# Turning attention weights two slots back instead of one in the opening of a top-k attention and MLP kernel

## The chip, the cores and the metric

The kernel runs on one core of a Trainium2 chip. The metric is the time of the device in microseconds, from the first instruction to the last, of one launch. Before the change it is 1626.51 us, the median of three runs (1626.12 to 1628.27). The profile is of another execution of the same kernel, whose span is 1627.3 us.

The core has five engines with a queue of instructions each: TensorE (PE in the profile; its weight loads are shown apart, as PEld), VectorE (DVE), ScalarE (ACT), GpSimd (POOL) and SyncE (SP, which here only starts transfers). [...]

## The reference

Two blocks, one after the other. First, attention that keeps the 32 largest scores of each row:

```python
B, H, S, D = 8, 8, 576, 64
scores = 1/sqrt(D) * q @ k.transpose(0, 1, 3, 2)
kth    = 32nd largest of each row
scores = where(scores >= kth, scores, -1e9) - max
attn   = exp(scores) / (sum(exp(scores)) + 1e-9)
x      = (attn @ v) as (4608 tokens, 512)
```

Then a two-layer MLP over the 4608 tokens, with w_in (512 x 2048) and w_out (2048 x 512):

```python
h   = x @ w_in
g   = h * sigmoid(1.702 * h)
out = g @ w_out
```

All of it is in 32-bit floats.

## The kernel before, in words

**Tiling.** A batch has 8 heads, taken as 4 pairs, and 576 rows, taken as four blocks of 128 and one of 64. A unit of attention work is 128 rows of two heads (the 64-row ends of two pairs share one unit). There are 18 units in a batch, so N = 144 in all; unit and slot have the same number n. The 128 lanes hold rows in the search, and the score row of a head has 576 columns.

**The stages of a unit**, by name and line:

- prepare (L199 to L208): TensorE transposes q and k, ScalarE copies the result out of PSUM.
- scores (L231): eight passes on TensorE into two PSUM tiles; copy_scores (L242): ScalarE copies them to SBUF, tile by tile.
- topk (L251, L254): VectorE finds the 32 largest of each row in four rounds of MAX8, with MATCH_REPLACE8 between them: 14 operations of two heads.
- bounds (L270, L271): GpSimd works out two small values from the largest and the 32nd largest.
- exponentials (L279, L281): ScalarE, two passes for each head; the second also sums the row.
- divide (L290, L292, L296): VectorE takes the reciprocal of the sum after the sixth operation of the next unit's search. For units below 11, GpSimd makes from it two diagonal matrices (the tile "by"), and turning then divides as it transposes.
- turn_main and turn_ends (L312, L315; L310 from unit 11 on): TensorE transposes the exponentials, in two main parts of 512 columns and one of 128; ScalarE copies each part to SBUF (L320).
- values (L342): TensorE multiplies by v; ScalarE copies the result (L354) into the token block xT. Four units complete a token block, which then is "ready".
- hidden (L385): a quarter of the first MLP layer of a ready block; tanh (L402) on ScalarE; gate (L418) on VectorE, or on GpSimd in the paired slots; project (L433): four matmuls of 512 columns into one accumulating PSUM tile, and every fourth time a copy and a store (L438, L440).

**The weights.** w_in and w_out come in 32 pieces. Each is rounded on its way: three ScalarE passes, "size" (L144), "low" (L147) and "sign" (L146), a shift on VectorE (L145), and two GpSimd operations ("finish", L140 and L141), which run in the next slot. Slots 0 to 11 handle 2, 2, 2, 3, 3, 3, 3, 4, 3, 3, 2 and 2 pieces. After that the weights are there.

**PSUM.** Turning, values and prepare take turns in the two buffers of one pool, ps_t. A unit's turning needs three and its values one. Scores use two tiles of another pool, with two buffers. The hidden layer has one buffer.

**The order.** The queues are written out by hand: the order in which the Python functions are called is the order of each engine's queue. The opening loads the first inputs; then slot(n) runs for n = 0 to 11; then two_slots(n) handles pairs from 12 on until all is searched; at the end slot is called for the rest of the MLP. In slot n before the change, ScalarE's queue holds, from the top: exponentials of unit n-1, copies of scores of n+1, sizes, tanh, two lows, copies of the turned unit n-1, further lows, the copy of values of n-1, signs. TensorE's queue holds in slots 3 to 7: scores of n+2, four warming products (stay_warm, L162, whose result is not used), turning of n-1, values of n-1, then four more warming products or, from slot 4 on, a hidden layer. From slot 8 on (settled) there is no warming, the projection goes around the turning, and scores of n+2 follow the values. In paired slots, turning and values are two units back.

Of the kernel before, what the change touches and what calls it, by code (L numbers as in the profile page):

```python
# [28 lines left out]
def kernel(  # L29
# [32 lines left out]
    NP = H // 2  # L62
# [6 lines left out]
    G = 4  # L69
# [9 lines left out]
    PROJECTS = 7  # L79
# [78 lines left out]
    def stay_warm(count, of=ident[:]):  # L158

        none = ps_p.tile([P, C], F32, name="none", tag="po")  # L160
        for i in range(count):
            nc.tensor.matmul(none[:, 0:P], lhsT=of, rhs=of, start=True, stop=True)  # L162
# [28 lines left out]
    def prepare(name, b, hp):  # L191
        src = loaded.pop((name, b, hp))


        before = 0 if name == "q" else TAIL
        dst = qkt.tile([P, S + before], F32, name=f"{name}_t")
        full = ps_t.tile([P, 512], F32, name="tp")
        for t in range(NF):
            nc.tensor.transpose(full[:, t * P : (t + 1) * P], src[:, t, :, :], ident[:])  # L199
        scale = SCALE if name == "q" else 1.0  # L200
        nc.scalar.mul(out=dst[:, before : before + FULL], in_=full[:], mul=scale)  # L201
        (qT if name == "q" else kT)[b, hp] = dst
        if name == "k":
            ends = ps_t.tile([P, 512], F32, name="tp")
            nc.tensor.transpose(ends[:, 0:P], loaded.pop(("ends", b, hp))[:], ident[:])
            nc.scalar.mul(out=qT[b, hp][:, FULL:S], in_=ends[:, 0:TAIL], mul=SCALE)
            for to in (0, before + FULL):
                nc.scalar.copy(out=dst[:, to : to + TAIL], in_=ends[:, TAIL:P])  # L208
# [12 lines left out]
    def scores(n):  # L221
        b, t, hps = slots[n]
        ps = [ps_s.tile([P, 2, 512], F32, name="s_ps") for _ in range(2)]
        if t < NF:
            parts = [(i, 0, slice(0, P), slice(t * P, (t + 1) * P)) for i in range(2)]
        else:
            parts = [(i, p, slice(p * TAIL, (p + 1) * TAIL), slice(FULL, S)) for i, p in ((0, 0), (1, 1), (0, 1), (1, 0))]
        for c in range(2):
            for i, p, rows, cols in parts:
                on = slice(i * D, (i + 1) * D)  # L230
                nc.tensor.matmul(  # L231
                    ps[i][rows, c, 0:HALF],
                    lhsT=qT[b, hps[p]][on, cols],
                    rhs=kT[b, hps[p]][on, FIRST[i] + c * HALF : FIRST[i] + (c + 1) * HALF],
                )
        st[n]["ps"] = ps

    def copy_scores(n):
        ps = st[n].pop("ps")
        sc = st[n]["sc"] = scp.tile([P, 2, S], F32, name="sc")  # L240
        for i in range(2):
            nc.scalar.copy(out=sc[:, i, :].rearrange("p (c k) -> p c k", c=2), in_=ps[i][:, :, 0:HALF])  # L242
# [22 lines left out]
    def bounds(n):  # L265

        top = st[n]["top"]
        cut = st[n]["cut"] = small.tile([P, 2], F32, name="cut")
        low = st[n]["low"] = small.tile([P, 2], F32, name="low")
        nc.gpsimd.tensor_scalar(cut[:], top[:, :, TOPK - 1], -1.0, None, op0=ALU.mult)  # L270
        nc.gpsimd.tensor_tensor(out=low[:], in0=top[:, :, TOPK - 1], in1=top[:, :, 0], op=ALU.subtract)  # L271

    def exponentials(n):

        sc, cut, low = st[n]["sc"], st[n]["cut"], st[n]["low"]
        pr = st[n]["pr"] = prp.tile([P, 2 * S], F32, name="pr")
        den = st[n]["den"] = small.tile([P, 2], F32, name="den")
        for i in range(2):
            nc.scalar.activation(sc[:, i, :], sc[:, i, :], AF.Prelu, bias=cut[:, i : i + 1], alpha=HUGE)  # L279
        for i in range(2):  # L280
            nc.scalar.activation(  # L281
                pr[:, i * S : (i + 1) * S], sc[:, i, :], AF.Exp, bias=low[:, i : i + 1],
                accum_out=den[:, i : i + 1],
            )
# [37 lines left out]
    def turn_main(n):  # L322
        for i in range(2):
            turn(n, i * NF, MAIN[i], NF)

    def turn_ends(n):

        turn(n, 2 * NF, FULL, 1)
# [68 lines left out]
    def tanh(aside):  # L397

        if to_gate:
            ph, g, rows = to_gate.pop()  # L400
            th = thp.tile([P, G, P], F32, name="th")
            nc.scalar.activation(th[:], ph[:], AF.Tanh, scale=0.851 / RAISE)  # L402
            if aside:
                h = raws.tile([P, G, P], F32, name="h", tag="raw")
                nc.scalar.copy(out=h[:], in_=ph[:])
                ph = h
            gated.append((th, ph, g, rows))

    def gate(aside):
        if not gated:  # L410
            return
        th, h, g, rows = gated.pop()
        gT = gtp.tile([P, G, P], F32, name="gT")
        if aside:
            nc.gpsimd.tensor_scalar(th[:], th[:], 1.0, None, op0=ALU.add)  # L415
            nc.gpsimd.tensor_tensor(out=gT[:], in0=th[:], in1=h[:], op=ALU.mult)  # L416
        else:
            nc.vector.scalar_tensor_tensor(  # L418
                out=gT[:], in0=th[:], scalar=1.0, in1=h[:], op0=ALU.add, op1=ALU.mult
            )  # L420
        to_project.append((gT, g, rows))
# [85 lines left out]
            load_piece(x)  # L507

    def slot(n):
        todo = later.pop(n, [])  # L510
        for fn, args in todo:
            if fn is not prepare:
                fn(*args)
        preparing = [args for fn, args in todo if fn is prepare]
        settled = n > PROJECTS
        aside = SETTLED < n < N
        before = 0 <= n - 1 < N
        if before:
            bounds(n - 1)
            exponentials(n - 1)  # L520
            copy_scores(n + 1)
        if n == 2:

            turn_main(0)
            turn_ends(0)
        some = [round_piece(x) for x in by_slot.get(n, [])] if n else early
        if n == 0:
            for piece in some:
                piece["low"]()
                piece["sign"]()  # L530
        else:
            for piece in some[:2]:
                piece["size"]()
        if not settled:
            for args in preparing:
                prepare(*args)
            scores(n + 2)
            if n == 2:
                values(0)
            stay_warm(4)  # L540
        if n > 0:
            for piece in some[2:]:
                piece["size"]()
        tanh(aside)
        for i, op in enumerate(topk(n) if n < N else [lambda: None] * 14):
            op()
            if i == 2:
                for _ in range(min(2, len(unfinished))):
                    finish_one()
            if i == 5:  # L550
                if before:
                    divide(n - 1)
                while unfinished:
                    finish_one()
            if i == 8 and not aside:
                gate(aside)
        for piece in some:
            piece["shift"]()
            unfinished.append(piece["finish"])
        if n == 0:  # L560
            return
        if aside:
            gate(aside)
        if settled:
            for args in preparing[:1]:
                prepare(*args)
        for piece in some[:2]:
            piece["low"]()
        going = settled and may_project(2 if n < N else 0)
        before = before and n > 1  # L570
        if going:
            project(range(G - 1))
        if before:
            turn_main(n - 1)
        if going:
            project(range(G - 1, G))
        if before:
            turn_ends(n - 1)
        for piece in some[2:]:
            piece["low"]()  # L580
        if before:
            values(n - 1)
        for piece in some:
            piece["sign"]()
        if settled and n + 2 < N:
            scores(n + 2)
            if n == SETTLED:
                copy_scores(n + 2)
        if settled:
            for args in preparing[1:]:  # L590
                prepare(*args)
        if not ready and not settled:
            stay_warm(4)
        hidden()

    def two_slots(n):
# [69 lines left out]
    with tc.manual_schedule():  # L666
        opening()
        for n in range(SETTLED + 1):
            slot(n)
        for n in range(SETTLED + 1, N + 1, 2):  # L670
            two_slots(n)
        n += 2
        while ready or to_gate or gated or to_project:
            slot(n)
            n += 1


# [28 lines left out]
```

## Time and profile before

| what | busy us | share of the span |
|---|---|---|
| TensorE, matmuls | 1592.9 | 98% |
| TensorE, weight loads | 1190.7 | 73% |
| VectorE | 1474.7 | 91% |
| ScalarE | 1154.3 | 71% |
| GpSimd | 749.1 | 46% |

These shares are means over two stages that differ. From 224 us to 1588 us TensorE is busy 43.8 to 44.0 us in every 44. In the single slots, from about 21 to 167 us, it is not: between 47 and 62 us it is busy 10.52 of 15 us, at a granted clock of 0.77 of the full one. The granted clock is a column of the views by time: 1.00 means that TensorE ran at full speed in that stretch.

The search of slot n (its first MAX8 on VectorE) starts at:

| slot | 1 | 2 | 3 | 4 | 5 | 6 | 7 | 8 | 9 | 10 | 11 | 12 |
|---|---|---|---|---|---|---|---|---|---|---|---|---|
| us | 21.65 | 32.22 | 42.80 | 57.17 | 71.87 | 87.80 | 101.48 | 116.08 | 129.44 | 141.97 | 153.15 | 165.89 |

In the chain of work, each line gives start, length and what the engine did, and each line was released by the one above it or follows it on its engine. A bracket at the end of a line of a timeline holds the idle time before the group, and what ended it.

### The profile page before, as it was taken

Reading aid. Unit: us, or ns where it says so; the run is one execution under the profiler, and the core shown is the slowest. Engines: PE = TensorE matmul, PEld = TensorE weight load, DVE = VectorE, ACT = ScalarE, POOL = GpSimd, SP = SyncE. Lnnn points to the kernel's source line nnn. Section 1 sums busy time; section 2 is a strip of 40 time slices with the busy share of each in tenths; the row PEclk is TensorE's granted clock in tenths of the full one; section 3 lists DMA queues with packets and bytes.
Section 4 is the critical chain, followed back from the end, with each engine's and each line's share of the span. In section 5 each row is a group of like instructions: output and inputs, shape, how many; then the busy total and the mean of one; then the engine's idle time right before and its main releaser. Section 6 shows DMA issues by size and latency. Waiting matters only on the chain.

```text
span 1627.3 us, 32166 instructions
## 1 busy us (share of the span) xinstructions
PE 1592.9 (98%) x12047; PEld 1190.7 (73%) x12047; DVE 1474.7 (91%) x3214; ACT 1154.3 (71%) x2445; POOL 749.1 (46%) x780
## 2 busy tenths in 40 slices
PE   7788999999999999999999999999999999999999
PEld 5676677777777777777777777777777777777776
DVE  7789999999999999999999998999999999999960
ACT  6788776777777777677777777677777777777761
POOL 3678444444444444444444444444444444444430
PEclk8889999999999999999999999999999999999999
DMA  7233001110001001110001100111000100000000
GB/s 231 96 118 102 22 22 30 29 44 15 22 15 44 22 22 30 29 37 22 22 15 29 29 22 10 30 29 44 15 22 15 44 22 23 22 7 8 8 7 14
DMA packets 100636, 56.61 MB, mean 35 GB/s; under 512 B 83584, under 2 KB 91776, under 8 KB 100480
## 3 DMA queue, kind: packets, MB, share of 16 engines
q1 hardware_dynamic: 100480, 54.55, 12.1%
q8 instruction: 95, 1.56, 0.4%
q14 instruction: 61, 0.50, 0.1%
HBM read 45.09 MB, written 9.44 MB: 34 GB/s over the span
## 4 chain that ended last, share of the span: by engine, by line
PE 90%; ACT 4%; DVE 3%; issue 1%; DMA 1%; POOL 0%; SPq 0%; ACTq 0%; POOLq 0%
PE ph L385 30%; PE po L433 29%; PE s_ps L231 10%; PE o L342 10%; PE tp L310 8%; DVE top L251 2%; PE tp L199 2%; DVE left L254 1%; PE tp L312 1%; ACT sc L242 1%; PE none L162 1%; ACT pr L281 1%; ACT raw L146 1%; ACT sc L279 0%; ACT pt L320 0%
## 5 line engine op out<-in xcount | busy, mean ns | idle before, releaser
L251 DVE MAX8 top<-left 128x8 f32<-128x576 f32 x864 | 610.1, 747 | 0.0
L433 PE MATMUL po<-wout,gT 128*128 128x512 f32 x1152 | 540.7, 593 | 2.4 <-POOL wout L141 1.7
L385 PEld LDWEIGHTS ph<-xT,win 128*128 128x128 f32 x4096 | 467.4, 192 | 41.4 <-issue 40.0
L385 PE MATMUL ph<-xT,win 128*128 128x128 f32 x4096 | 484.7, 277 | 0.0
L254 DVE MATCH_REPLACE8 left<-top,left 128x576 f32<-128x576 f32 x576 | 423.4, 743 | 0.0
L299 POOL TENSOR_SCALAR pr<-pr,rden 128x576 f32<-128x576 f32 x133 | 230.0, 1730 | 348.8 <-ACT th L402 340.3
L433 PEld LDWEIGHTS po<-wout,gT 128*128 128x128 f32 x1152 | 197.3, 191 | 146.7 <-issue 142.0
L320 ACT COPY pt<-tp 128x512 f32<-128x512 f32 (+1 forms) x432 | 193.1, 481 | 157.0 <-PE tp L310 139.2
L415 POOL TENSOR_SCALAR th<-th 128x512 f32<-128x512 f32 x131 | 196.0, 1496 | 220.8 <-ACT th L402 220.8
L279 ACT ACTIVATE sc<-sc,cut 128x576 f32<-128x576 f32 x288 | 208.0, 773 | 123.4 <-POOL cut L270 123.3
L242 ACT COPY sc<-s_ps 128x576 f32<-128x576 f32 x288 | 169.7, 643 | 70.8 <-PE s_ps L231 70.6
L281 ACT ACTIVATE pr<-sc,low 128x576 f32<-128x576 f32 x288 | 219.1, 764 | 0.0
L310 PEld LDWEIGHTS tp<-ident,pr 128*128 128x128 f32 x1197 | 143.1, 141 | 102.5 <-issue 56.3
L254 DVE MATCH_REPLACE8 left<-top,sc 128x576 f32<-128x576 f32 x288 | 211.6, 742 | 0.0
L251 DVE MAX8 top<-sc 128x8 f32<-128x576 f32 x288 | 202.1, 743 | 10.3 <-ACT sc L242 10.3
L231 PE MATMUL s_ps<-k_t,q_t 64*128 64x288 f32 (+1 forms) x1280 | 188.1, 436 | 14.2 <-ACT sc L242 13.2
L310 PE MATMUL tp<-ident,pr 128*128 128x128 f32 x1197 | 174.2, 273 | 0.3 <-ACT k_t L201 0.3
L416 POOL TENSOR_TENSOR gT<-th,h 128x512 f32<-128x512 f32 x131 | 167.4, 1278 | 10.9
L342 PE MATMUL o<-pt,v_l 128*64 128x128 f32 (+1 forms) x2560 | 157.4, 266 | 2.6 <-ACT pt L320 1.8
L231 PEld LDWEIGHTS s_ps<-k_t,q_t 64*128 64x128 f32 (+1 forms) x1280 | 102.4, 179 | 74.2 <-issue 40.3
L342 PEld LDWEIGHTS o<-pt,v_l 128*64 128x64 f32 x2560 | 130.1, 137 | 32.4 <-ACT pt L320 17.4
L270 POOL TENSOR_SCALAR cut<-top 128x2 f32<-128x2 f32 x144 | 39.8, 277 | 234.1 <-DVE top L251 231.3
(55 smaller groups left out, 1188.1 us busy)
## 6 DMA issues: line engine op xcount, KB each, us to landing
q_l<-in_q_dram SPq DMA_DIRECT2D x64, 128.0 KB, 3.0
k_l<-in_k_dram SPq DMA_DIRECT2D x64, 128.0 KB, 3.0
raw<-in_moe_w_in_dram SPq DMA_DIRECT2D x16, 512.0 KB, 4.9
v_l<-in_v_dram SPq DMA_DIRECT2D x32, 256.0 KB, 3.0
raw<-in_moe_w_out_dram SPq DMA_DIRECT2D x16, 512.0 KB, 3.3
out_dram<-ob SPq DMA_DIRECT2D x32, 256.0 KB, 2.3
ends<-in_q_dram SPq DMA_DIRECT2D x32, 32.0 KB, 2.5
ends<-in_k_dram SPq DMA_DIRECT2D x32, 32.0 KB, 2.6
```

The source lines that it names most:

```text
L231: nc.tensor.matmul(ps[i][rows, c, 0:HALF], lhsT=qT[b, hps[p]][on, cols], rhs=kT[b, hps[p]][on, FIRST[i] + c * HALF : FIRST[i] + (c + 1) * ...
L251: nc.vector.max(top[:, i, 8 * r : 8 * r + 8], (left if r else sc)[:, i, :])
L254: nc.vector.match_replace(left[:, i, :], top[:, i, 8 * r : 8 * r + 8], (left if r else sc)[:, i, :], LOWEST)
L279: nc.scalar.activation(sc[:, i, :], sc[:, i, :], AF.Prelu, bias=cut[:, i : i + 1], alpha=HUGE)
L281: nc.scalar.activation(pr[:, i * S : (i + 1) * S], sc[:, i, :], AF.Exp, bias=low[:, i : i + 1], accum_out=den[:, i : i + 1],)
L299: nc.gpsimd.tensor_scalar(pr[:, S : 2 * S], pr[:, S : 2 * S], rden[:, 1:2], None, op0=ALU.mult)
L310: nc.tensor.transpose(tp[:, c * P : (c + 1) * P], pr[:, at], ident[:])
L320: nc.scalar.copy(out=to, in_=tp[:, 0 : blocks * P])
L342: nc.tensor.matmul(o[j * D : (j + 1) * D, 0 : cols.stop - cols.start], lhsT=main[:, j, c, :] if c < NF else tail[:, j, :], rhs=pt[:, j * N ...
L385: nc.tensor.matmul(ph[:, i, :], lhsT=win[:, c, f * P : (f + 1) * P], rhs=xT[:, c, :], start=(c == 0), stop=(c == CC - 1),)
L415: nc.gpsimd.tensor_scalar(th[:], th[:], 1.0, None, op0=ALU.add)
L433: nc.tensor.matmul(po[:], lhsT=gT[:, i, :], rhs=wout[:, f, :], start=(f == 0), stop=(f == FC - 1))
```

## The change

In the single slots, turning and values are moved from unit n-1 to unit n-2, as in the paired slots. Unit n-1's exponentials go first in ScalarE's queue with no condition, then copies of scores of n+1, tanh, and at once the copies of the turned unit n-2. The sizes come behind these. On TensorE the projection and then the scores of n+2 follow the turning; values of n-2 come after the scores. All lows and signs come behind the copy of values. Before the values there are four warming products in slots 2 to 5 only, and the warming of slots 0, 1, 6 and 7 goes away; four more come at the end of slots 1 to 5. The gate stands one place later in VectorE's queue. The end of the kernel gets a small function of its own, last_slot, with the same instructions. The aim is that the exponentials never stand behind work of the same slot, and that turning uses results that are a slot old.

The diff, cut to its core:

```diff
     def slot(n):
...
-        if before:
-            bounds(n - 1)
-            exponentials(n - 1)
-            copy_scores(n + 1)
-        if n == 2:
-            turn_main(0)
-            turn_ends(0)
...
+            bounds(n - 1)
+            exponentials(n - 1)
+            copy_scores(n + 1)
+            tanh(False)
+            if n > 1:
+                turn_main(n - 2)
+                turn_ends(n - 2)
+            for piece in some:
                 piece["size"]()
-        if not settled:
-            for args in preparing:
-                prepare(*args)
-            scores(n + 2)
-            if n == 2:
-                values(0)
-            stay_warm(4)
...
-            if i == 8 and not aside:
-                gate(aside)
+            if i == 9:
+                gate(False)
         for piece in some:
             piece["shift"]()
             unfinished.append(piece["finish"])
+        if n > PROJECTS and may_project(2):
+            project(range(G))
+        if n < NP:
+            for args in preparing:
+                prepare(*args)
+        scores(n + 2)
+        if n == SETTLED:
+            copy_scores(n + 2)
         if n == 0:
             return
...
-        for piece in some[:2]:
-            piece["low"]()
-        going = settled and may_project(2 if n < N else 0)
-        before = before and n > 1
-        if going:
-            project(range(G - 1))
-        if before:
-            turn_main(n - 1)
-        if going:
-            project(range(G - 1, G))
-        if before:
-            turn_ends(n - 1)
-        for piece in some[2:]:
-            piece["low"]()
-        if before:
-            values(n - 1)
+        idle = not ready and n < PROJECTS
+        if idle and n > 1:
+            stay_warm(4)
+        if n > 1:
+            values(n - 2)
+        for piece in some:
+            piece["low"]()
+        if n >= NP:
+            for args in preparing:
+                prepare(*args)
         for piece in some:
             piece["sign"]()
-        if settled and n + 2 < N:
-            scores(n + 2)
-            if n == SETTLED:
-                copy_scores(n + 2)
...
+        if idle:
             stay_warm(4)
         hidden()
```

More of the change, by code (lines that the diff above doesn't have):

```diff
@@ L514, in slot @@
         preparing = [args for fn, args in todo if fn is prepare]
-        settled = n > PROJECTS
-        aside = SETTLED < n < N
-        before = 0 <= n - 1 < N
-        if before:
-            bounds(n - 1)
-            exponentials(n - 1)
-            copy_scores(n + 1)
-        if n == 2:
-            turn_main(0)
-            turn_ends(0)
         some = [round_piece(x) for x in by_slot.get(n, [])] if n else early
@@ L531, in slot @@
         else:
-            for piece in some[:2]:
-                piece["size"]()
-        if not settled:
-            for args in preparing:
-                prepare(*args)
-            scores(n + 2)
-            if n == 2:
-                values(0)
-            stay_warm(4)
-        if n > 0:
-            for piece in some[2:]:
-                piece["size"]()
-        tanh(aside)
-        for i, op in enumerate(topk(n) if n < N else [lambda: None] * 14):
+            bounds(n - 1)
[6 more added lines that the diff above has]
+            for piece in some:
+                piece["size"]()
+        for i, op in enumerate(topk(n)):
             op()
@@ L550, in slot @@
             if i == 5:
-                if before:
+                if n > 0:
                     divide(n - 1)
@@ L559, in slot, with last_slot @@
             unfinished.append(piece["finish"])
+        if n > PROJECTS and may_project(2):
[6 more added lines that the diff above has]
+            copy_scores(n + 2)
         if n == 0:
             return
[L562 to L565, printed above, removed]
-                prepare(*args)
-        for piece in some[:2]:
-            piece["low"]()
-        going = settled and may_project(2 if n < N else 0)
-        before = before and n > 1
-        if going:
-            project(range(G - 1))
-        if before:
-            turn_main(n - 1)
-        if going:
-            project(range(G - 1, G))
-        if before:
-            turn_ends(n - 1)
-        for piece in some[2:]:
-            piece["low"]()
-        if before:
-            values(n - 1)
+        idle = not ready and n < PROJECTS
[7 more added lines that the diff above has]
+            for args in preparing:
+                prepare(*args)
         for piece in some:
             piece["sign"]()
-        if settled and n + 2 < N:
-            scores(n + 2)
-            if n == SETTLED:
-                copy_scores(n + 2)
[L589 to L592, printed above, removed]
-            stay_warm(4)
+        if idle:
+            stay_warm(4)
+        hidden()
+    def last_slot():
+        tanh(False)
+        gate(False)
+        if may_project(0):
+            project(range(G))
         hidden()
@@ L671 @@
             two_slots(n)
-        n += 2
         while ready or to_gate or gated or to_project:
-            slot(n)
-            n += 1
+            last_slot()
 _INS = ["q", "k", "v", "moe_w_in", "moe_w_out"]
```

## The prediction

> **What bounds the kernel now.** I read four views: the page, the chain of work that ended last (slots 1 to 11), TensorE's timeline there, and the busy time by slot. "Slot" is one of the single slots 0 to 11, which end near 167 us; from there the slots run in pairs.
>
> ```profile
> PE 1592.9 (98%) x12047; PEld 1190.7 (73%) x12047; DVE 1474.7 (91%) x3214; ACT 1154.3 (71%) x2445; POOL 749.1 (46%) x780
> ```
>
> Over the whole span TensorE is full: from 224 to 1588 us it is busy 43.8 to 44.0 us in each 44. A pair of slots takes 21.3 us there (the second hidden layer of a pair starts at 231.36, 252.69, 273.98). The change can't touch that. What it can move is the moment at which TensorE has done all of the single slots and of the first pair: 189.87 us now, the end of the last hidden layer of pair 12. I call it E. Both orders of instructions are the same after E, so the new time is the old one plus the shift of E, less what TensorE still waits after E now.
>
> Before E, the slots are bound by a ring through ScalarE and TensorE. The chain, slot 6 into 7 (start, us, what):
>
> ```profile
> 88.61 1.72 ACT raw L146 x3
> 90.33 0.71 ACT sc L279 x2
> ...
> 91.55 1.61 ACT pr L281 x4
> 93.17 0.53 ACT sc L242
> ...
> 93.74 2.10 PE s_ps L231 x8
> 95.84 2.01 PE none L162 x8
> 97.84 2.15 PE tp L312 x16
> ...
> 100.02 0.59 ACT pt L320
> ...
> 100.66 1.34 PE o L342 x20
> 102.02 0.27 ACT xT L354
> 102.29 1.74 ACT raw L146 x3
> ```
>
> The reader sees one lap: signs, exponentials, a copy of scores, then on TensorE scores, warming products and turning, a copy, values, a copy, signs. A lap is 13.7 us (88.61 to 102.29). VectorE needs less: 9.9 us for a search with its division (slot 13, 177.16 to 187.07, nothing else in it), 0.33 for each shift, 0.6 for a gate, so 11.5 with three pieces. The waits from 45 to 122 us say the same:
>
> ```profile
> DVE some L290 <- ACT pr L281: 13.3, 6, 3.7
> PE s_ps L231 <- ACT sc L242: 13.2, 5, 4.3
> ```
>
> VectorE waits 13.3 us in six slots for the exponentials, TensorE 13.2 us in five for a copy of scores that stands behind them. And those waits slow TensorE: after a gap of 1.7 us the scores take 2.10 us, and 1.24 without a gap; the eight warming passes take 2.08 or 1.16.
>
> ```profile
> 40.60 1.16 PE L162 MATMUL none<-ident 128*128 128x128 f32 x8
> 93.74 2.10 PE L231 MATMUL s_ps<-k_t,q_t 64*128 64x288 f32 x8 [1.68 <-ACT sc L242]
> 95.77 2.08 PE L162 MATMUL none<-ident 128*128 128x128 f32 x8
> 127.76 1.24 PE L231 MATMUL s_ps<-k_t,q_t 64*128 64x288 f32 x8
> ```
>
> By slot, the granted clock shows it (second number: us; then PE, PEld, DVE, ACT, POOL, clock). Slots 3 and 4 run at 0.77, 5 to 7 at 0.87 or 0.88, slot 8, the first with a projection, at 1.00:
>
> ```profile
> 47.00:62.00 15.00, 10.52 (x64) 8.64 (x64) 11.44 (x25) 10.39 (x22) 7.78 (x9) 0.77 0.22 70
> 104.00:118.00 14.00, 12.00 (x93) 10.18 (x92) 11.45 (x26) 12.65 (x26) 9.74 (x11) 0.88 0.46 135
> 118.00:130.00 12.00, 10.85 (x78) 7.34 (x78) 10.71 (x24) 11.45 (x24) 11.28 (x12) 1.00 0.55 167
> ```
>
> **What the Trainium skill says.** "TensorE: Matmul & The Clock Gate", Part 1 (the HAM clock gate): the array's clock is halved when a free-running window of about 3.4 us was idle, and given back after a busy one. The trace agrees in kind (0.77 of 15 us is 6.9 us at half, two windows; 0.88 of 14 is 3.4, one), and goes further: a gap of 1.7 us, half a window, was enough. The same page, section on the 32x32 sub-arrays: ScalarE and VectorE are strict first in, first out, and only weight loads overtake on TensorE. The trace agrees: the sign pieces at 88.61, for which only GpSimd waits, held up the exponentials. So the order of the queue is what counts here.
>
> **The change, part by part.** In slot n ScalarE now does: exponentials(n-1), copies of scores(n+1), tanh, copies of the turned blocks of n-2, sizes, copy of values, lows, signs. TensorE does: turning(n-2), projection, scores(n+2), warming, values(n-2), hidden layer.
>
> *Removed:* turning's 2.15 us from the lap, since its two main parts need nothing of this slot (divisor and exponentials are a slot old) and run while ScalarE is at its exponentials. Of the warming passes the lap now holds a 4-product one in slots 2 to 5 only.
>
> *Added to the lap, first:* turning has three parts and two buffers in PSUM. The third (turn_ends) needs the buffer that the first copy of turned blocks frees, and that copy now stands behind exponentials, copies of scores and tanh. TensorE's queue stops there, with projection, scores and values behind it; the copy of values is behind those, and lows and signs behind that copy. So projection (four of L433, 0.86 each, 3.44 us) and scores come between two ScalarE stages in slots 8 to 10. Now they are off the lap there.
>
> *Added, second:* the lows. Three of 0.575 us (1.72 for three signs, the lows alike) stood in time that ScalarE spent waiting; now they follow the copy of values, in front of the next exponentials: 1.7 us a slot.
>
> The lap at full clock: exponentials 2.85 (62.06 to 64.91 in slot 4), copies of scores 1.05, tanh 0.48 (from slot 6), first copy of turned blocks 0.59, turn_ends with its release 0.45, [projection 3.44], scores 1.2, [warming 1.05], values 1.35, copy 0.3, lows and signs 1.15 for each piece. Slot 2: 11.1; slots 3 to 5: 12.3; 6: 11.7; 7 (four pieces): 12.9; 8 and 9: 15.2; slot 10: GpSimd sets it, as its projection needs a piece finished in that very slot: bounds 1.2, two finishes of 2.6, divisors 1.2, a third finish 2.6 is 10.2, then 0.86 + 1.2 + 1.35 + 0.3 + 2.3 = 16.2.
>
> Exponentials start now at 32.4, 46.9, 62.1, 76.5, 90.2, 103.9, 118.2, 129.8, 142.2, 155.3 in slots 2 to 11. Full clock would give 43.5 in slot 3, 80.4 in slot 6, 105.0 in slot 8, 151.4 in slot 11.
>
> *The clock.* The trace has no lap of this order, so its cost is bounded from both sides. TensorE's queue stands still from the end of turning's main parts to turn_ends. In slots 3 to 5: values end 3.75 before the next lap, then 1.05 warming and 1.9 turning, then it waits to 4.5 into the lap: 5.3 us idle. In slots 6 to 10 the hidden layer (3.6) makes it 3 us. Both are above the 1.7 us that already halved the clock. Low end: nothing; high end: the whole ring at half. I take what such gaps cost now: scores 2.1 to 2.8 instead of 1.2, warming 2.0 instead of 1.05, a part of values: 3.0 in slot 2 (the clock is 0.65 there now), 2.5 in 3 to 5; one window of 3.4 us, 1.7 of it lost, in 6 and 7, and 1.8 in 8 and 9; in slot 10 GpSimd hides it. Laps then: 14.1, 14.8 three times, 13.4, 14.6, 17.0, 17.0, 16.2. From 32.4: slot 3 at 46.5, slot 6 at 90.9, slot 8 at 118.9, slot 11 at 169.1, against 155.3 now. Slots 2 to 7 break even, slots 8 to 10 lose 14 us, and VectorE waits for the exponentials in each.
>
> *Slot 11 and pair 12.* One turning, one set of values and one hidden layer move from the single slots into pair 12: 1.85 + 0.45 + 1.35 + 3.6 = 7.2 us on TensorE. From the exponentials of slot 11 to E, TensorE's row: 5.0 until turn_ends, 0.45, scores 2.1, values 1.35, preparation 0.6, hidden 3.6, preparation 0.7, seven of L433 6.0 and 0.7 for the evacuation (both seen now at 174), turning 1.85, 0.86, 0.45, hidden 3.6, 2.6, turning 0.9, 0.96, then 1.2 + 2.7 + 1.2 + 3.6: 40.4. Now it is 34.5. So E goes to 169.1 + 40.4 = 209.5, 19.6 later.
>
> *Given back:* now the first two pairs after E take 22.9 and 22.25 us where 21.3 is normal, since they wait for VectorE's search and the exponentials after it. With E that late VectorE is ahead (pair 12 gives it a lead of 6 us that it lacks now), so 2.5 us return. Net: 19.6 - 2.5 = 17; the time 1644.
>
> *At nothing:* the end of the kernel (the last slots do the same in the same order); the gate one place later, under search; GpSimd's pieces elsewhere, 10 us in laps of 13 to 17; loads, which ask for buffers freed a slot ahead.
>
> **The rivals.**
> - *The ring closes below VectorE's need* (what the change aims at). For it: now VectorE waits 13.3 us. Slots 1 to 11 at its own need put slot 11's search at 133.0, its exponentials at 134, E at 173.5, and the time at 1610. Against: each lap above exceeds VectorE's even at full clock. 0.05.
> - *The clock holds.* Then slot 11 at 151.4, E (scores 0.9 shorter) at 190.9, 1 later, less 2.5: 1625, no change. For it: slots with projection ran at 1.00. Against: those had gaps under 0.9 us, these have 3. 0.12.
> - *Forecast:* ring with one to two slow windows a slot, 1644. 0.65.
> - *Slow longer:* two windows in each of slots 6 to 9 and values at half in 3 to 5: 1.7 x 4 + 0.9 x 3 more, 1654. 0.18.
>
> **How the numbers follow.** Likeliest: 1644. The low end leaves out the first rival and most of the second (between them and the forecast is a clock that drops in some slots only): 1629. The high end takes in the fourth case: 1656. Within 0.2% is 1623.3 to 1629.8: the second rival less its tails and a little of the forecast's, 0.10; faster: the first and a tail of the second, 0.08; slower 0.82.
>
> **What would show it.** Right: VectorE's waits for the exponentials at the division grow in slots 8 to 10; in the chain turn_ends (L315) follows L320 and is followed by L433, L231, L342, L354 and six of L147 and L146; the clock stays below 1.00 in slots 8 to 10; slot 11's exponentials near 169; E near 209; afterwards pairs of 21.3 us at once. Wrong: if turn_ends does not wait for the copy, if TensorE has no gap over 1 us in slots 6 to 10, or if the lows and signs finish before the bounds of their slot are out.

## The result and the profile after

The changed kernel takes 1641.76 us (median of four runs, 1634.91 to 1642.77), against 1627.24 us before: a ratio of 1.008, 95% interval 1.0052 to 1.0109. Timed again among the experiments it took 1641.36 us, ratio 1.0079 (1.0063 to 1.0094). It is slower by about 0.8%. The profiled runs have spans of 1639.6 us and 1627.3 us, 12.3 us apart, and all of these 12.3 us lie ahead of 203 us.

The busy times have hardly changed, so no engine has more work:

```profile
PE 1590.0 (97%) x12031; PEld 1185.1 (72%) x12031; DVE 1474.0 (90%) x3213; ACT 1153.8 (70%) x2446; POOL 750.7 (46%) x782
```

The second hidden layer of pair 12 starts at 186.20 us before and at 198.97 us after:

```profile
186.20 3.84 PE L385 MATMUL ph<-xT,win 128*128 128x128 f32 x32
198.97 3.84 PE L385 MATMUL ph<-xT,win 128*128 128x128 f32 x32
```

From that start to the end of the span it is 1441.1 us before and 1440.6 after. In the traces of all the experiments below it is 1440.5 to 1441.0 too, so the opening alone decides.

The chain of work of the changed kernel, slot 8 (start, us, what):

```profile
113.16 0.71 ACT sc L279 x2
...
114.38 1.62 ACT pr L281 x4
116.00 1.06 ACT sc L242 x2
117.06 0.49 ACT th L402
117.55 0.48 ACT pt L320
...
118.07 0.69 PE tp L315 x4
118.76 4.90 PE po L433 x8
123.67 1.17 PE s_ps L231 x8
124.84 1.27 PE o L342 x20
...
126.12 0.27 ACT xT L354
126.39 1.72 ACT raw L147 x3
128.11 1.70 ACT raw L146 x3
```

This is the lap that the prediction put together, in its order: turn_ends (L315) after the first copy of turned blocks, then projection, scores and values, then six low and sign passes ahead of the next exponentials (129.70). It takes 16.7 us; slot 8 took 11.6 before (118.17 to 129.79), where turn_ends waited 0.38 us for a copy:

```profile
126.03 0.44 PE L315 MATMUL tp<-by,pr 128*64 128x128 f32 x4 [0.38 <-ACT pt L320]
```

The waits from 31 to 203 us after the change (us in total, times, longest):

```profile
PE tp L315 <- ACT pt L320: 33.7, 10, 5.3
DVE some L290 <- ACT pr L281: 28.0, 9, 5.1
POOL by L296 <- PE tp L315: 20.3, 8, 3.4
```

Before, the first of these was 0.7 us and the third 0.6. VectorE's wait for the exponentials has about doubled instead of going away; this was its line before:

```profile
DVE some L290 <- ACT pr L281: 14.5, 8, 3.7
```

Busy time and clock by slot after the change (slots 3, 7 and 8; columns as in the prediction):

```profile
42.20:57.20 15.00, 10.05 (x67) 7.91 (x66) 14.39 (x33) 10.43 (x23) 9.23 (x10) 0.77 0.23 71
98.70:113.00 14.30, 11.13 (x92) 9.58 (x92) 12.90 (x30) 12.74 (x26) 10.85 (x12) 0.88 0.42 131
113.00:129.70 16.70, 12.42 (x81) 8.28 (x80) 14.30 (x28) 11.04 (x23) 11.67 (x12) 0.90 0.53 161
```

Slot 8, at a clock of 1.00 before, is now at 0.90: TensorE stands still for 4.28 us, and then the projection takes 4.97 us, where a projection without a wait before it, in the first experiment below, takes 3.60:

```profile
118.07 0.69 PE L315 MATMUL tp<-by,pr 128*64 128x128 f32 x4 [4.28 <-ACT pt L320]
118.69 4.97 PE L433 MATMUL po<-wout,gT 128*128 128x512 f32 x8
```

### The profile page after: what moved, and what is told of

It is laid out like the page before. It is cut to its first block, busy times and chain, and to the rows that moved or that the text cites. A ratio compares the mean times of both kernels' runs of the same rounds, so it can differ in the third digit from the quotient of the medians.

```text
span 1639.6 us, 32136 instructions
## 1 busy us (share of the span) xinstructions
PE 1590.0 (97%) x12031; PEld 1185.1 (72%) x12031; DVE 1474.0 (90%) x3213; ACT 1153.8 (70%) x2446; POOL 750.7 (46%) x782
## 3 DMA queue, kind: packets, MB, share of 16 engines
q1 hardware_dynamic: 100480, 54.55, 11.7%
## 4 chain that ended last, share of the span: by engine, by line
PE 91%; ACT 5%; DVE 2%; issue 1%; POOL 0%; DMA 0%; SPq 0%; POOLq 0%; ACTq 0%
PE ph L385 31%; PE po L433 30%; PE s_ps L231 10%; PE o L342 10%; PE tp L310 8%; PE tp L199 2%; ACT sc L242 1%; ACT pr L281 1%; ACT raw L147 1%; ACT raw L146 1%; DVE top L251 1%; DVE left L254 1%; ACT sc L279 0%; PE none L162 0%; PE tp L315 0%
## 5 line engine op out<-in xcount | busy, mean ns | idle before, releaser
L342 PEld LDWEIGHTS o<-pt,v_l 128*64 128x64 f32 x2560 | 131.6, 138 | 31.9 <-ACT pt L320 13.5
L290 DVE TENSOR_SCALAR some<-den 128x2 f32<-128x2 f32 x144 | 46.3, 322 | 102.2 <-ACT pr L281 102.2
```

Source lines behind the costliest of these rows:

```text
L342: nc.tensor.matmul(o[j * D : (j + 1) * D, 0 : cols.stop - cols.start], lhsT=main[:, j, c, :] if c < NF else tail[:, j, :], rhs=pt[:, j * N ...
```

## The experiments

Times are medians; each ratio is to the kernel before, run on the same chip at the same time. "Changed" is the changed kernel.

| run | what | us | ratio (95%) |
|---|---|---|---|
| e1 | changed, projection first | 1626.78 | 0.9998 (0.9989 to 1.0006) |
| e2 | changed, lows early | 1628.51 | 1.0011 (1.0002 to 1.0019) |
| e3 | changed, gaps filled | 1632.32 | 1.0030 (1.0018 to 1.0041) |
| e4 | changed, projection and scores first, lows early | 1625.78 | 0.9991 (0.9984 to 0.9998) |
| e5 | before, unit 10 left to pair 12 | 1628.34 | 1.0016 (1.0008 to 1.0024) |
| e6 | e1 and e2, two divisor buffers | 1620.73 | 0.9963 (0.9951 to 0.9976) |
| e7 | e6, gaps filled, no warming ahead of values | 1614.43 | 0.9928 (0.9916 to 0.9940) |
| e8 | changed, two divisor buffers | 1636.67 | 1.0067 (1.0053 to 1.0081) |
| e9 | changed, again | 1641.36 | 1.0079 (1.0063 to 1.0094) |
| e10 | before, warming moved ahead of scores | 1615.83 | 0.9932 (0.9920 to 0.9944) |
| e11 | e7 with one divisor buffer | 1615.74 | 0.9932 (0.9919 to 0.9945) |

**e1, the projection out of the lap.**

```diff
+            if n > PROJECTS and may_project(2):
+                project(range(G))
             if n > 1:
                 turn_main(n - 2)
                 turn_ends(n - 2)
...
-        if n > PROJECTS and may_project(2):
-            project(range(G))
```

> The changed kernel with the projection put ahead of the turning on TensorE (first in slots 9 to 11, as slot 8 has only two gated tiles so early). Ring theory: the projection's 3.44 us leave the lap and fill the idle time before turn_ends, so the clock stays full there as well. Laps of slots 8, 9 and 10 fall from 16.7, 16.8 and 15.7 to about 13.2, 11.8 and 10.7 us: 13.5 us less, about 1628. Rival (the loss comes from the unit that moved into pair 12, and from warming that is gone): nothing of that is touched, so it stays within 2 us of the changed kernel, about 1640.

Measured: 1626.78, some 15 us less than the changed kernel. Slot 8 has no projection in this kernel. In slots 9 and 10 the projection now fills the gap, and turn_ends waits 0.96 us or not at all:

```profile
121.70 3.60 PE L433 MATMUL po<-wout,gT 128*128 128x512 f32 x8
128.04 0.44 PE L315 MATMUL tp<-by,pr 128*64 128x128 f32 x4 [0.96 <-ACT pt L320]
139.81 0.44 PE L315 MATMUL tp<-by,pr 128*64 128x128 f32 x4
```

Laps of slots 8 to 10: 12.8, 11.55 and 11.2 us, 13.6 us less together, as the sum said. The rival falls: the projection's place alone is worth about what the whole change lost. In this trace slots 3 to 7, which the edit doesn't touch, are 3.5 us shorter too; slot 6 ran at full clock there. The clock can differ like this from run to run with no edit to TensorE's queue at all (see the paragraph on the clock below).

**e2, the lows out of the lap.**

```diff
+        for piece in some:
+            piece["low"]()
         if n > 1:
             values(n - 2)
-        for piece in some:
-            piece["low"]()
```

> The changed kernel with the low passes put ahead of the copy of values in ScalarE's queue, where ScalarE idles 1.5 to 6.4 us a slot. Ring theory: 0.575 us for each of 26 pieces leaves the laps of slots 2 to 10, 15 us in all, of which VectorE's own need in slots 2 and 6 keeps about 1: 14 us less, about 1628. Rival (ScalarE's order behind the values is off the path): within 2 us of the changed kernel, about 1640.

Measured: 1628.51, 13 us less. Slots 3 to 7 take 12.0, 13.3, 13.5, 11.0 and 12.7 us (15.0, 14.4, 14.1, 13.0, 14.4 in the changed kernel). Slot 8 gains nothing in this trace: it takes 16.6 us, as its projection runs slower, 6.55 us.

**e3, the clock.**

```diff
                 turn_main(n - 2)
+                if n in FILL:            # 3 to 5: 18, 6: 8, 7: 9
+                    stay_warm(FILL[n])
                 turn_ends(n - 2)
```

> The changed kernel with 18 idle products on TensorE between turn_main and turn_ends in slots 3 to 5, 8 in slot 6 and 9 in slot 7, to fill the gap there. Clock theory (gaps before turn_ends halve the clock, which costs 2.5 us in slots 3 to 5 and 1.5 in 6 and 7): the clock of slots 3 to 7 goes to 0.95 or more and the laps to 12.3, 11.7 and 12.9: about 10 us less, 1631. Rival (order alone, the clock costs nothing): no less than the changed kernel, 1641 or above.

Measured: 1632.32, 9 us less. The order is the same, only the gap is filled. Slots 4, 5 and 7 of this kernel:

```profile
55.50:67.70 12.20, 10.87 (x103) 9.73 (x102) 11.50 (x26) 10.60 (x22) 9.92 (x11) 1.00 0.41 131
67.70:79.80 12.10, 10.79 (x102) 9.65 (x102) 11.51 (x26) 10.48 (x22) 9.88 (x10) 1.00 0.40 130
91.40:104.10 12.70, 11.59 (x111) 10.57 (x110) 12.67 (x29) 12.64 (x27) 11.19 (x11) 1.00 0.52 166
```

The clock is 1.00, and laps are 12.1 to 12.2, then 11.5 and 12.7 us, where the prediction's sum at full clock said 12.3, 11.7 and 12.9. Slots 8 to 10, which aren't filled, take 16.65, 16.8 and 15.7 us, as in the changed kernel.

**e4, all moves at once: the expectation failed.** The diffs of e1 and e2, and `scores(n + 2)` between turn_main and turn_ends.

> The changed kernel with projection first, scores ahead of turn_ends and lows early. Ring theory: what is left of the lap is exponentials 2.85, copies of scores 1.05, tanh 0.48, first copy of turned blocks 0.59, turn_ends 0.45, values 1.35, copy 0.3, signs 1.7: 8.8 us (11 with a slow clock), below VectorE's 11.5, so the slots are bound by VectorE's search (or by TensorE's own 11.9 in slots with a projection). Exponentials of slot 11 at 136 to 140, all of TensorE's work through pair 12 done at 177 to 182: 21 to 26 us less than the changed kernel, 1615 to 1620, below the kernel before. Rival (two units back costs in pair 12 what it gains in the slots): no faster than the kernel before, 1627 or above.

Measured: 1625.78, no better than e1 alone by more than a microsecond. The trace shows two things that the sum of 8.8 us left out. First, ScalarE's own work: exponentials 2.85, copies 1.05 and 1.27, tanh 0.48, copy of values 0.27 and three passes on each of three pieces, 5.2, are 11.1 us in any order, and 12.9 with four pieces. It also waited 10.6 us in ten slots for turn_ends, which now stood behind slow scores. Second, slot 8 (this kernel's GpSimd and ScalarE):

```profile
111.35 1.18 POOL L296 TENSOR_SCALAR by<-ident,rden 128x128 f32<-128x128 f32 x2 [4.20 <-PE tp L315]
...
118.65 0.22 POOL L270 TENSOR_SCALAR cut<-top 128x2 f32<-128x2 f32 x1
```

```profile
118.91 1.44 ACT L279 ACTIVATE sc<-sc,cut 128x576 f32<-128x576 f32 x2 [2.08 <-POOL cut L270]
```

The divisors have one buffer, and turning of n-2 reads it in the slot in which GpSimd wants to write n-1's. GpSimd waits 4.20 us for turn_ends, the pieces slip behind it, and the bounds, which could be made once the search had ended at 113.9, come at 118.65. ScalarE, free since 116.8, waits 2.08 us for them.

**e6 and e7, repaired.** e6 is e1 and e2 with a second divisor buffer (odd units borrow the output's, idle until pair 12), and scores behind turn_ends. e7 adds the fill (14, 14, 14, 8, 8 and 9 in slots 3 to 8) and drops the warming ahead of values.

```diff
-            by = st[n]["by"] = dgp.tile([P, 2, P], F32, name="by")
+            by = st[n]["by"] = osp.tile([P, 2, P], F32, name="by", tag="ob") if n % 2 else dgp.tile([P, 2, P], F32, name="by")
```

> The changed kernel with projection first and lows early (scores stay behind turn_ends), and with a second buffer for the divisors (tile by), so that GpSimd need not wait for turn_ends of the unit before. Theory after the third experiment of this kind missed (with all three moves, slot 8 waited 2 us for bounds that stood in GpSimd's queue behind the divisors, and ScalarE's copy of the last turned block waited for the slow scores): no wait for bounds in slot 8, exponentials of slot 11 near 139.5, the time 1617 to 1620. Rival (ScalarE's own work, 11.1 us in a slot with three pieces, and a slow clock bound it in any order): as with all three moves, 1624 to 1627.

> As e6_two_divisors, and without the warming in front of values, and with 14 idle products ahead of turn_ends in slots 3 to 5, 8 in slots 6 and 7 and 9 in slot 8. Theory: the clock is full in slots 3 to 8 and the laps fall to what ScalarE and VectorE need (11 to 11.5, 12.9 in slot 7), 6 us less than e6_two_divisors: 1611 to 1614. Rival (the clock no longer counts once the ring is short): the same as e6_two_divisors.

Measured: 1620.73 and 1614.43. After slot 8 of e6 ScalarE waits only 0.60 us for bounds (2.08 us in e4); its slots 3 to 5 still run 13.4, 13.5 and 12.0 us with a slow clock. e7's slots 3 to 5 take 10.9 to 11.0 us, and the clock hardly matters there any more. Slots 3 and 4 of e7:

```profile
42.63:53.55 10.92, 9.20 (x75) 8.02 (x74) 10.88 (x26) 10.49 (x22) 7.41 (x9) 0.84 0.32 98
53.55:64.46 10.91, 10.46 (x101) 9.44 (x100) 10.88 (x26) 10.57 (x21) 9.97 (x11) 1.00 0.37 113
```

The lap is the same at 0.84 and at 1.00: VectorE and ScalarE are busy for nearly all of it. So e7's theory missed in part: not every slot got the full clock. e7 is 6.3 us faster than e6, but it both fills the gap and takes the warming out of the lap, and no run separates the two. Both kernels end a little above what was hoped for.

**e8, e9 and e11, what the divisors' wait is worth.**

> The changed kernel with nothing but the second buffer for the divisors. In the changed kernel GpSimd waits 20.3 us in eight slots for turn_ends before it writes the divisors. Theory: that wait is off the path there, since the lap is longer than GpSimd's 10 us of work, so it goes away and the time stays within 2 us of the changed kernel, 1639 to 1643. Rival (it holds up bounds and so exponentials): 5 us less or more, 1636 or below.

> The changed kernel, not edited, timed again beside the others. Theory of the clock ([...]where it falls in a lap decides how much of scores, values and projection runs slow): the times spread over several us, 1634 to 1643, with a median of 1637 to 1642, and the kernel with the second divisors buffer (1635.1 to 1642.2) isn't told apart from it. Rival (the second buffer is worth 5 us): all runs at 1640 to 1643.

> As e7_clock_too but with the single buffer for the divisors that the changed kernel has. Theory (with a short ring GpSimd's queue is on the path, since bounds stand in it behind divisors that wait for turn_ends): 2 to 4 us more than e7_clock_too, 1616 to 1618. Rival (GpSimd has room, 10 us of work in laps of 11 to 13): the same, 1614 to 1615.

Measured: e8 1636.67 (1635.11 to 1642.2); e9 1641.36 (1635.52 to 1642.9); e11 1615.74, against 1614.43 for e7. The ranges of e8 and e9 cover each other, with more of e8's runs at the low end. In the short ring the difference is 1.3 us, and the ranges again overlap. So the largest new wait on GpSimd, 20.3 us in total and gone from e8's trace, is worth between nothing and 5 us; the runs don't settle it further. In e8's trace the clock fell in other slots than in the changed kernel's (see below), which alone can move the time.

**e5, the unit that moved into pair 12.**

```diff
-        before = before and n > 1
+        before = before and 1 < n < SETTLED
```

> The kernel before, with turning and values of unit 10 left out of slot 11, so that pair 12 does them, as in the changed kernel. Theory (what counts is when TensorE has done all of its work through pair 12, and from slot 11 on it is close to full in the kernel before): the same work is done later in a stretch that is full anyway, so the time stays within 2 us of the kernel before. Rival (the 6 us that slot 11 and pair 12 took longer in the changed kernel are the price of one unit moving there): 5 to 6 us more, 1632.

Measured: 1628.34, 2.2 us more: neither theory's number. The 16 runs fall into two groups: twelve took 1626.4 to 1629.5 us, four 1631.9 to 1632.9, which is what the rival said. The trace is of a run of the upper group. From the exponentials of slot 11 (153.75) to E (193.24) it takes 39.5 us, where the kernel before takes 34.5. TensorE waits there for weights that GpSimd hasn't finished, and the projections after the waits run slowly:

```profile
167.30 1.12 PE L433 MATMUL po<-wout,gT 128*128 128x512 f32 x2 [0.86 <-POOL wout L141]
169.91 2.08 PE L433 MATMUL po<-wout,gT 128*128 128x512 f32 x2 [1.49 <-POOL wout L141]
172.68 4.65 PE L433 MATMUL po<-wout,gT 128*128 128x512 f32 x6 [0.69 <-ACT ob L438]
```

The same six passes take 2.84 us in the changed kernel. So pushing one unit into pair 12 lengthens this stretch by 5 us in the trace and costs 2.2 us in the median. That this unit is also what makes the stretch 6 us longer in the changed kernel fits, but isn't shown by itself.

**e10, the kernel before with nothing but its warming moved ahead, and more of it.**

```diff
+            if n in FILL:                # 3, 4: 14; 5 to 7: 6
+                stay_warm(FILL[n])
             scores(n + 2)
...
-            stay_warm(4)
+            if n not in FILL:
+                stay_warm(4)
```

> The kernel before, with the four warming products of slots 3 to 7 moved from behind the scores to ahead of them, as 14 products in slots 3 and 4 and 6 in slots 5 to 7, to fill the gap in which TensorE waits for the copy of scores. Theory: the lap of the kernel before loses the warming (2.0 us) and the slow clock (0.9 in scores, 0.35 in turning), down to VectorE's and ScalarE's own 11 to 11.5 us (13 in slot 7): 2 us less in each of slots 3 to 6 and 1 in slot 7, 9 to 11 us in all: 1616 to 1618. Rival (turning one slot back is what makes the ring long, and the clock is a small matter): no more than 3 us less, 1624 or above.

Measured: 1615.83, 10.6 us less than before. Two windows of this kernel, 47 to 62 us as in the prediction, and 62 to 85 us:

```profile
47.00:62.00 15.00, 13.42 (x107) 10.72 (x106) 13.70 (x32) 14.36 (x30) 10.08 (x12) 1.00 0.33 105
62.00:85.00 23.00, 21.03 (x184) 17.92 (x183) 22.09 (x52) 21.76 (x45) 19.45 (x20) 1.00 0.42 139
```

From 62 to 85 us the clock was 0.78 before. Slots 3 to 7 take 11.2, 11.3, 11.6, 11.9 and 12.7 us instead of 15.2, 14.5, 13.7, 13.7 and 14.3, and VectorE waits 3.2 us for exponentials where it waited 14.3. Two things changed at once: the warming, some 2 us a slot, left the lap, and the clock rose. No run separates them, but even at full clock the scores take 1.77 us here, not 1.24 (slot 4; lines of this kernel are numbered one higher):

```profile
59.99 1.77 PE L232 MATMUL s_ps<-k_t,q_t 64*128 64x288 f32 x8 [0.93 <-ACT sc L243]
60.52 0.78 PEld L232 LDWEIGHTS s_ps<-k_t,q_t 64*128 64x128 f32 x6 [0.25 <-ACT sc L243]
```

The second line shows why: the later passes wait once more, for the copy of the second score tile. This version, e6, e7 and e11 beat both kernels.

## Why the prediction was right, and where it was off

**That the opening decides, through the end of pair 12: right.** E moved by 12.8 us and the span by 12.3.

**The lap: right, within 0.7 us in each of slots 3 to 10.** Exponentials of slots 2 to 12 start at 31.14, 42.16, 57.19, 71.56, 85.65, 98.69, 113.05, 129.70, 146.47, 162.15 and 173.08. The laps of slots 3 to 10 are 15.0, 14.4, 14.1, 13.0, 14.4, 16.7, 16.8 and 15.7; the prediction had 14.8 three times, 13.4, 14.6, 17.0, 17.0 and 16.2. Its three parts were tested one by one: the projection in the lap (e1), the lows (e2), the clock (e3). Each gave back 9 to 15 us. They don't add up, since VectorE's and ScalarE's own 11 us are met first (e4, e7).

**The clock: right in kind, and in size for this trace.** The prediction rested on "TensorE: Matmul & The Clock Gate" of the Trainium skill. Slots with gaps of 2.2 to 5.3 us ran at 0.76 to 0.90, and filling them in slots 3 to 7 (e3) brought 1.00 and the laps of the sum. Another section of that page, "HAM oscillation", gives the rule of no gaps above about 3.4 us. It is not sharp enough here: three gaps of 1.7 us in the kernel before were followed by a slow clock (the warming passes took 2.07 to 2.08 us, not 1.16), while in slot 11 of the changed kernel one of 1.94 us, and in slot 8 of e1 one of 3.58 us, were followed by scores at the full 1.24 us. Even the same gap in the same slot does not decide. Slot 6 of the changed kernel, then of e8, in which TensorE's queue is the same:

```profile
90.67 0.69 PE L315 MATMUL tp<-by,pr 128*64 128x128 f32 x4 [2.23 <-ACT pt L320]
91.29 2.29 PE L231 MATMUL s_ps<-k_t,q_t 64*128 64x288 f32 x8
```

```profile
91.80 0.44 PE L315 MATMUL tp<-by,pr 128*64 128x128 f32 x4 [2.23 <-ACT pt L320]
92.17 1.24 PE L231 MATMUL s_ps<-k_t,q_t 64*128 64x288 f32 x8
```

Slots 6 and 7 of e8 took 11.5 and 12.7 us, at a clock of 1.00, and its slot 8 took 18.15. So it is in part luck that the sizes hit slot by slot. Part 1 of the page says that the clock's window runs free of the program; such a window would do this, and so would explain why the changed kernel's own runs spread over 7 to 8 us. That was not tested by itself.

**The slow scores: misread.** The prediction took the 2.10 us of the scores in the kernel before, against 1.24, as the price of the clock. As e10 shows, they take 1.77 there at full clock, since they wait for two copies; only about 0.3 us was the clock. In the changed kernel the scores follow turn_ends, both copies are done by then, and they still took 2.2 to 2.3 us in slots 3 to 7: so the price that the prediction put in was about right, from a line that did not show it.

**Slot 2: mis-sized.** The prediction took 3.0 us for a slow clock there, from the kernel before. The lap took 11.0 us, its full-clock sum: after a gap of 1.13 us the scores took 1.24 us. The exponentials of slot 2 also began 1.3 us earlier than before; in the experiments the first exponentials start anywhere from 20.3 to 22.0 us whatever the order, so this is not the change's. Together these are 4.4 of the 7 us by which slot 11 came earlier than forecast (162.15, not 169.1); the rest are a few tenths in each of slots 4 to 10. So slots 2 to 7 did not break even, as forecast: slot 8 began 5 us earlier than before (113.05, not 118.17), and slots 8 to 10 lost 12 us. The prediction says 14 for these, but its own laps make 13.1.

**Slot 10: right in size, wrong in cause.** GpSimd finished the piece at 155.9 and would have let the projection end near 156.7; the slow projection ended at 157.2, so the clock set the lap, by half a microsecond.

**Slot 11 and pair 12: right in total, with luck.** 40.5 us from the exponentials to E, forecast 40.4. The scores took 1.24 us, where the forecast had 2.1, and a wait of 1.20 us came in that it didn't have:

```profile
178.51 1.12 PE L433 MATMUL po<-wout,gT 128*128 128x512 f32 x2 [1.20 <-POOL wout L141]
```

**"Given back": wrong.** The prediction read pairs of 22.9 and 22.25 us after E as waiting for VectorE, and expected 2.5 us back. By the starts of the second hidden layer they are 22.7 and 22.35 us, and the longest wait of TensorE in them was 0.3 us, for a copy of k. After the change the same pairs take 22.3 and 22.35 us with TensorE at work throughout: they hold more preparation of q and k than the later ones. Only 0.5 us came back. This error and the one in slot 2 have opposite signs, which is why the total (17 forecast, 14.5 between the medians, 12.3 between the traces) came out as close as it did; that is luck.

**Not foreseen:** that GpSimd would wait for turn_ends because the divisors have one buffer. It isn't in the changed kernel's chain of work, whose lap is longer anyway; in e4 it was seen to hold up ScalarE.

## What to carry to other kernels

Follow each queue once around before moving work back a step: here the results that were "a slot old" still ended in a part that waited for this slot's copy, because three parts shared two buffers, and everything behind it on TensorE came into the lap. Put passes that nobody waits for, and products that only keep the clock up, ahead of an instruction that waits, not behind it: with the warming products alone, in the old order, that gave 10.6 us. And when a ring gets short, check each engine's own sum before promising more.

## What the runs showed of the hardware

A gap in TensorE's work can cost more than its own length, by what it does to the next few microseconds: in the changed kernel, after gaps of 3 to 4 us, the projections took 4.97 to 5.40 us, and 3.60 without a gap (e1); scores took 2.2 to 2.3 us after gaps of 2.2 to 5.3 us, and 1.24 in slots without a slow clock. How long the gap was did not say whether the clock fell: after 1.7 us it did, after 3.58 us it did not, and after 2.23 us in the same slot it did in one run and not in another. In e8 a gap of 4.30 us was followed by a projection of 6.47 us, one of 3.08 us by one of 3.70.
